# A Fourier filter and a channel MLP on one Trainium2 core: the residual operand turned by transposing DMAs instead of by TensorE and VectorE

## The chip, the cores and the metric

The kernel runs on one core of one Trainium2 chip. The metric is the device time of one execution in microseconds, and the median over runs is compared. The engines are called PE (TensorE), PEld (its weight loads), DVE (VectorE), ACT (ScalarE), POOL (GpSimd) and SP (SyncE, which here only issues DMAs).

## The reference

For each of 8 batches of 3136 positions and 256 channels:

```
X  = rfft(x, axis=1)                    # over the 3136 positions
y  = irfft(X * (filt_r + 1j*filt_i))    # one filter per frequency and channel
u  = y + ((y^T @ U) @ V)^T              # a low-rank (32) mixing over the positions
out = u + relu(u @ w_ch1) @ w_ch2       # w_ch1: 256 x 1024, w_ch2: 1024 x 256
```

Inputs and output are float32; the kernel computes in float16 with float32 sums.

## The kernel before, in words

The transform of length 3136 is split as 49 x 64 and done by matmuls. Each batch passes four stages, and then its rows pass the MLP:

- Stage 1 (`f1`, line 241; `f1_turned` for batches 0 and 1): matmuls of x with the table `ws`. ACT evicts to a tile `asb` (line 255, four buffers), and SP stores it to DRAM as `ct1` and `ct0` (lines 257 and 258).
- Stages 2 and 3 (`mid`, line 319): SP loads `ct1` and `ct0` as `a2` and `a20` (`load_a2`, lines 328 and 331), a matmul gives pz (line 384), DVE multiplies it by the filter (lines 392 to 397), a second matmul gives pe (line 345), ACT evicts it to `e3` (line 355), and SP stores it to DRAM as `ct2` (line 364, in the page as `ct<-e`).
- The rows: `load_e2` (line 412) loads `ct2` back as the 96 rows `eb`, the operand of stage 4, in three parts of two halves. `rank` (line 419) works out the low-rank term, which DVE copies into the first 32 rows of `eb` (line 438).
- Stage 4 (`s4`, line 445): matmuls of `eb` with `sv` (line 456) give u with channels on the partitions, `ut` (128 x 2 x 3136, two buffers); DVE and ACT evict it (lines 463 and 461).
- The MLP goes over the 25,088 rows of all batches in 49 groups of 512. `mm1` (line 484) gives eight blocks of the hidden layer, which ACT evicts with the relu (line 491). `mm2` (line 538) sums them over the hidden layer into a bank `pc` with rows on the partitions (line 544).

All but batch 0's stages is dealt over the MLP's steps. A step is one `mm1` block of group n and one half of an `mm2` block of group n-1; there are eight steps a group. The list `plan` names, for each step, the generators that are advanced by one piece behind it. Each engine takes its instructions in this order, and so does SP with its DMAs: one that waits holds all behind it.

```
for n, gr in enumerate(groups):
    for t in range(8):
        mm1(gr, t)
        if n:
            mm2(groups[n - 1], t)
        for gen in plan[8 * n + t]:
            next(gen, None)
```

S[b] is the first step of the group in which batch b begins: 0, 48, 96, 144, 192, 240, 288, 336, with 392 as the end. For batch b, z = S[b], and e = z - 17, z - 20 or z - 22 (b = 1, 2 to 5, 6 and 7) is where stage 3 ends. The row loads are at e - 5, e - 4 and e + 1, `rank` goes from e to e + 6, and stage 4 from e + 8 to z - 2.

The MLP's residual needs u with rows on the partitions, and `ut` has channels there. There are two ways in the kernel, chosen by `turned`:

- Groups 0 to 37: TensorE adds it, by eight matmuls of a block of `ut` with the identity into the same bank (`residual`, line 536), two more where two batches meet inside a block. DVE then copies the bank to `och` (line 561).
- Groups 38 to 48 (`FIRST_TURNED = 38`): `turn_u` transposes `ut` on DVE in blocks of 32 x 32 (line 515), SP stores the result to DRAM in four DMAs (line 520) and loads it as `tur` (line 524, in a buffer of the x tiles). DVE then adds it while it evicts the bank (line 557).

POOL's queue stores `och` to the output, and loads x for a later batch.

Of the kernel before, what the change touches and what calls it, by code (L numbers as in the profile page):

```python
# [10 lines left out]
F16 = mybir.dt.float16  # L11
# [3 lines left out]
NB = 8  # L15
# [3 lines left out]
DM = 256  # L19
# [1 line left out]
NH = 1024  # L21
GT = 512
NG = NB * SEQ // GT
FIRST_TURNED = 38

# [53 lines left out]
def kernel(  # L81
# [11 lines left out]
    nc = tc.nc  # L93
# [15 lines left out]
    sb = ctx.enter_context(tc.tile_pool(name="sb", bufs=1))  # L109
    ps = ctx.enter_context(tc.tile_pool(name="ps", bufs=2, space=bass.MemoryType.PSUM))  # L110

    def bank(tag, name, dtype=F32):

        return ps.tile([128, 512 if dtype == F32 else 1024], dtype, tag=tag, bufs=4 if tag == "z" else 2, name=name)

    def dram(t, off, dims):
        return bass.AP(tensor=t, offset=off, ap=[list(d) for d in dims])
# [88 lines left out]
    tu = eb[0:RANK, 0:12, :].rearrange("p r d -> p (r d)")  # L206
# [34 lines left out]
    def f1(b):  # L241
        for c in range(4):
            t = xt[b, c].rearrange("p (j d) -> p j d", d=DM)
            asb = sb.tile([98, 8, DM], F16, tag="asb", bufs=4, name="asb")
            for half in range(2):
                for i in range(2):
                    pf = bank("z", "pf")
                    for s in range(2):
                        j = 4 * half + 2 * i + s
                        nc.tensor.matmul(pf[0:98, 256 * s:256 * s + 256],  # L250
                                         ws[:, (8 * c + j) * 98:(8 * c + j + 1) * 98], t[:, j, :],
                                         start=(s == 0), stop=True, skip_group_check=True)
                    dst = asb[:, 4 * half + 2 * i:4 * half + 2 * i + 2, :]
                    src = pf[0:98].rearrange("p (j d) -> p j d", d=DM)
                    nc.scalar.copy(dst, src)  # L255
                    if half and i:
                        nc.sync.dma_start(dram(ct1[b], 8 * c * 96 * DM, [[DM, 96], [96 * DM, 8], [1, DM]]), asb[0:96])
                        nc.sync.dma_start(dram(ct0[b], 8 * c * DM, [[32 * DM, 2], [1, 8 * DM]]),
                                          asb[96:98].rearrange("p j d -> p (j d)"))
                    yield  # L260
# [58 lines left out]
    def mid(b, tag="z"):  # L319
        a2 = {}  # L320

        def load_a2(g):
            if b < 2:
                a2[g] = turn(b, g)
                return
            if g == 3:
                t = a20[b % 2]
                nc.sync.dma_start(t[0:64], ct0[b].ap())
            else:
                t = sb.tile([128, 8, DM], F16, tag="a2", bufs=3, name="a2")  # L330
                nc.sync.dma_start(t, dram(ct1[b], 8 * g * DM, [[24 * DM, 128], [1, 8 * DM]]))
            a2[g] = t
# [34 lines left out]
            spread_filters(0)  # L367
        for g in (0, 3, 1, 2) if b > 1 else (0, 3):
            load_a2(g)
        todo = []  # L370
        first_at = 2 if b < 2 else 6
        for i, ks in enumerate(PAIRS[:first_at] + [(0,)] + PAIRS[first_at:]):
            n = len(ks) * DM
# [7 lines left out]
            if ks[0]:  # L381
                src = a2[(ks[0] - 1) // 8]
                k = (ks[0] - 1) % 8
# [3 lines left out]
            o = 512 if ks[0] % 4 == 3 else 0  # L387
# [93 lines left out]
    def utv(b):  # L481
        return ut[b].rearrange("p h q r -> p h (q r)")
# [9 lines left out]
        gr.h.append(h)  # L492

    def turned(gr):
        return gr.n >= FIRST_TURNED

    def turn_u(gr):

        t = sb.tile([128, 4, 4, 2, 32], F16, tag="asb", bufs=4, name="tu")
        for dh in range(2):
            for b, t0, o, n in gr.seg:
                j, z = o // 32, (o + n) // 32
                while j < z:

                    k = min(z, j + 4 - j % 4) if j % 4 or z - j < 4 else z - z % 4
                    src = utv(b)[:, dh, t0 + 32 * j - o:t0 + 32 * k - o]
                    if k - j < 4:
                        dst = t[:, j % 4:j % 4 + k - j, j // 4, dh, :]  # L510
                        src = src.rearrange("p (c e) -> p c e", e=32)
                    else:
                        dst = t[:, :, j // 4:k // 4, dh, :].rearrange("p c g e -> p g c e")
                        src = src.rearrange("p (g c e) -> p g c e", c=4, e=32)
                    nc.vector.transpose(dst, src)
                    j = k
            yield
        td = nc.dram_tensor(f"tu_{gr.n}", (128, 4 * DM), F16, kind="Internal")
        for a in range(4):
            nc.sync.dma_start(dram(td, DM * a, [[4 * DM, 32], [128 * DM, 4], [1, DM]]),  # L520
                              t[32 * a:32 * a + 32].rearrange("i c g h e -> i c (g h e)"))
        yield
        gr.tu = sb.tile([128, 4, 4, 2, 32], F16, tag="x", bufs=4, name="tur")
        nc.sync.dma_start(gr.tu.rearrange("p a g h e -> p (a g h e)"), td.ap())
        yield

    def residual(gr, o, i):
        last = []
        for b, t0, so, n in gr.seg:
            a, z = max(so, 128 * i), min(so + n, 128 * i + 128)  # L530
            for dh in range(2):
                if a < z:
                    p = a - 128 * i
                    last.append((o[p:p + z - a, 128 * dh:128 * dh + 128], utv(b)[:, dh, t0 + a - so:t0 + z - so], dh))
        for d, w, dh in last:
            nc.tensor.matmul(d, w, idn, start=False, stop=(dh == 1), skip_group_check=True)  # L536

    def mm2(gr, t):
        i, half = t // 2, t % 2
        if t % 4 == 0:  # L540
            gr.pc = bank("o", "pc")
        o = gr.pc[:, 256 * (i % 2):256 * (i % 2) + 256]
        for tt in range(4 * half, 4 * half + 4):
            nc.tensor.matmul(o, gr.h[tt][:, 128 * i:128 * i + 128], w2sb[:, tt, :],  # L544
                             start=(tt == 0), stop=(tt == 7 and turned(gr)), skip_group_check=True)
        if half and not turned(gr):
            residual(gr, o, i)

        parts = {3: (0, 1), 5: (2,), 7: (3,)} if gr.n == NG - 1 else {3: (0, 1), 7: (2, 3)}
        if t not in parts:  # L550
            return
        if t == 3:
            gr.och = sb.tile([128, 4, DM], F32, tag="och", bufs=2, name="och")
        a, n = parts[t][0], len(parts[t])
        dst, src = gr.och[:, a:a + n, :], gr.pc[:, 256 * (a % 2):256 * (a % 2 + n)]
        if turned(gr):
            nc.vector.tensor_add(dst.rearrange("p g (h a e) -> p (g h) a e", h=2, a=4),  # L557
                                 src.rearrange("p (f a e) -> p f a e", a=4, e=32),
                                 gr.tu[:, :, a:a + n].rearrange("p a g h e -> p (g h) a e"))
        else:  # L560
            nc.vector.tensor_copy(dst, src.rearrange("p (j d) -> p j d", d=DM))  # L561
        if gr.n == NG - 1:
            nc.sync.dma_start(dram(out.tensor, (gr.n * GT + 128 * a) * DM, [[DM, 128], [128 * DM, n], [1, DM]]), dst)
        elif t == 7:
            nc.gpsimd.dma_start(dram(out.tensor, gr.n * GT * DM, [[DM, 128], [128 * DM, 4], [1, DM]]), gr.och)  # L565
# [3 lines left out]
    plan = [[] for _ in range(8 * NG)]  # L569

    def deal(gen, count, a, z):
        for i in range(count):
            plan[max(0, int(a + i * (z - a) / count))].append(gen)
# [6 lines left out]
    mids = [mid(0, "o")] + [mid(b) for b in range(1, NB)]  # L580
    ranks = [rank(b) for b in range(NB)]
    s4s = [s4(b) for b in range(NB)]
    turns = [turn_u(gr) for gr in groups]
# [47 lines left out]
    def loads(b, part):  # L631
        load_e2(b, part)
        yield

    for b in range(1, NB):
        a, z = S[b - 1], S[b]
        e = z - (17 if b == 1 else 20 if b < 6 else 22)
        deal(mids[b], 13, a + {1: 8, 2: -3}.get(b, -5), e - 4)
        deal(mids[b], 4, e - 4, e)
        for p, at in enumerate((e - 5, e - 4, e + 1)):  # L640
            plan[at].append(loads(b, p))
        deal(ranks[b], 6, e, e + 6)
        deal(s4s[b], 16, e + 8, z - 2)
        if b == 1:
            deal(f1s[1], 12, 1, 8)
        if b + 1 < NB:
            for c in range(4):
                plan[a + (9 + 2 * c if b == 1 else 1 + 4 * c)].append(later_x(b + 1, c))
            deal(f1s[b + 1], 16, a + (21 if b == 1 else 10), z - (13 if b == 1 else 20))

    for gr in groups:
        if turned(gr):
            for i in range(4):
                plan[8 * gr.n + (0, 1, 2, 5)[i]].append(turns[gr.n])
    for n, gr in enumerate(groups):
        for t in range(8):
            mm1(gr, t)
# [36 lines left out]
```

## Time and profile before

| | |
|---|---|
| median of 3 runs | 514.82 us (513.02 to 515.63) |
| the profiled execution | 516.74 us |
| its span in the profile | 514.9 us |
| TensorE busy, granted clock | 490.8 us (95%), 0.997 |
| DVE, ACT, POOL busy | 365.4, 377.0, 80.6 us |
| DMA: moved, mean rate | 93.99 MB, 183 GB/s |

Busy shares are of the span. A matmul's duration is the time that it takes to pass through the array, and the next begins before it ends, so the pace of matmuls is read from their starts. A wait is put down to what came last; an engine's idle time costs something only where another waits for it. A DMA is shown as issued; it lands some microseconds later, and its packets run on 16 DMA engines that all queues share.

### The profile page before, as it was taken

The numbers are of one execution on the slowest core, as the hardware profiler recorded it, in microseconds if no ns is written. First come the engines' busy times: TensorE is split into PE (matmuls) and PEld (weight loads), VectorE is DVE, ScalarE is ACT, GpSimd is POOL, SyncE is SP. The second block draws the span as 40 slices with busy tenths as digits, with TensorE's granted clock in tenths as the row PEclk, the third lists the DMA queues.
The fourth block names the chain that finished last, engine by engine and source line by source line (L and its number), as shares of the span: only waits on it lengthen the run. The fifth ranks groups of instructions, "written<-read, shape, count | busy, mean of one in ns | idle before, by whom it ended". The sixth has DMA issues, their size and how long they took to land.

```text
span 514.9 us, 11918 instructions
## 1 busy us (share of the span) xinstructions
PE 490.8 (95%) x4762; PEld 349.8 (68%) x4762; DVE 365.4 (71%) x496; ACT 377.0 (73%) x704; POOL 80.6 (16%) x122
## 2 busy tenths in 40 slices
PE   4886899999999999999999999999999999999997
PEld 4545566776777777777767777677667766676665
DVE  5886599479847986679747986679846897863432
ACT  6874779867986689667986689667895677666663
POOL 6662010012001120002001120002001000011100
PEclk9998999999999999999999999999999999999999
DMA  8987926847777386827877386836977136654454
GB/s 192 170 210 177 174 80 178 271 168 181 215 227 249 77 188 195 293 118 187 208 226 251 75 190 203 276 129 168 224 230 239 55 103 204 206 159 145 131 163 163
DMA packets 75312, 93.99 MB, mean 183 GB/s; under 512 B 5731, under 2 KB 58403, under 8 KB 75256
## 3 DMA queue, kind: packets, MB, share of 16 engines
q1 hardware_dynamic: 60552, 51.65, 33.1%
q0 software_dynamic: 14704, 41.58, 31.5%
q8 instruction: 37, 0.61, 0.5%
q14 instruction: 19, 0.16, 0.1%
HBM read 58.09 MB, written 50.66 MB: 211 GB/s over the span
## 4 chain that ended last, share of the span: by engine, by line
PE 80%; DMA 10%; DVE 4%; ACT 2%; POOL 1%; issue 1%; SPq 1%; POOLq 0%; DVEq 0%; ACTq 0%
PE pc L544 30%; PE phh L488 29%; PE pu L456 5%; PE pf L250 4%; PE pe L345 4%; PE pz L384 3%; DMA ct<-e 3%; PE pc L536 3%; DVE uv L392 2%; DMA eb<-ct 2%; DMA w2sb<-in_moe_w_ch_dram 2%; DMA x<-in_x_dram 2%; DMA fab<-in_filt_i_dram 1%; PE ph L423 1%; POOL x L128 1%
## 5 line engine op out<-in xcount | busy, mean ns | idle before, releaser
L491 ACT ACTIVATE h<-phh 128x512 f16<-128x512 f32 x392 | 235.9, 603 | 85.3 <-PE phh L488 83.8
L544 PE MATMUL pc<-w2sb,h 128*128 128x256 f16 x1568 | 233.8, 272 | 1.4 <-DMA w2sb<-in_moe_w_ch_dram 0.9
L488 PE MATMUL phh<-ut,w1sb 128*128 128x512 f16 (+7 forms) x896 | 233.3, 352 | 0.4 <-DVE ut L463 0.4
L544 PEld LDWEIGHTS <-h 128*128 128x128 f16 x1568 | 151.6, 97 | 92.2 <-issue 1.8
L392 DVE TENSOR_TENSOR uv<-pz,fab 128x1024 f16<-128x1024 f32 (+1 forms) x104 | 120.7, 1178 | 12.6 <-PE pz L384 10.5
L565 POOL DMA_DIRECT2D out_dram<-och x48 | 39.0, 813 | 402.7 <-DVE och L561 327.1
L488 PEld LDWEIGHTS <-w1sb 128*128 128x128 f16 x896 | 78.9, 97 | 19.8 <-issue 1.5
L561 DVE COPY och<-pc 128x512 f32<-128x512 f32 x76 | 52.3, 689 | 44.7 <-PE pc L536 43.5
L355 ACT CAST e<-pe 128x512 f16<-128x512 f32 x96 | 56.5, 591 | 19.4 <-PE pe L345 18.5
L463 DVE CAST ut<-pu 128x392 f16<-128x392 f32 x92 | 48.5, 558 | 19.6 <-PE pu L456 17.3
L255 ACT CAST asb<-pf 98x512 f16<-98x512 f32 x96 | 57.2, 598 | 0.2
L438 DVE COPY eb<-h 32x4096 f16<-32x4096 f16 x32 | 38.2, 1232 | 14.2 <-ACT h L435 14.1
L456 PE MATMUL pu<-sv,eb 97*128 97x49 f16 x1024 | 40.5, 187 | 5.4 <-DMA eb<-ct 5.4
L557 DVE TENSOR_TENSOR och<-pc,tur 128x512 f32<-128x512 f32 (+1 forms) x23 | 15.3, 667 | 40.4 <-PE pc L544 38.7
L345 PE MATMUL pe<-uv,m 128*128 128x512 f16 (+1 forms) x117 | 41.3, 371 | 2.4 <-DVE uv L392 1.3
L456 PEld LDWEIGHTS <-eb 97*128 97x128 f16 x1024 | 37.6, 98 | 7.2 <-issue 4.7
L536 PE MATMUL pc<-idn,ut 128*128 128x128 f16 (+1 forms) x310 | 41.9, 219 | 0.0
L384 PE MATMUL pz<-a,m 128*128 128x512 f16 x96 | 36.2, 379 | 1.3 <-DVE a L311 1.0
L250 PE MATMUL pf<-x,ws 98*98 98x256 f16 x192 | 36.6, 273 | 0.0
L536 PEld LDWEIGHTS <-ut 128*128 128x128 f16 (+1 forms) x310 | 29.6, 98 | 4.0 <-issue 0.6
L396 DVE TENSOR_TENSOR uv<-uv 64x1024 f16<-64x1024 f16 (+1 forms) x49 | 30.9, 630 | 1.7
L397 DVE TENSOR_TENSOR uv<-uv 64x1024 f16<-64x1024 f16 (+1 forms) x49 | 30.7, 627 | 0.7
(80 smaller groups left out, 262.7 us busy)
## 6 DMA issues: line engine op xcount, KB each, us to landing
out_dram<-och POOLq DMA_DIRECT2D x48, 512.0 KB, 4.1
ct<-e SPq DMA_DIRECT2D x47, 256.0 KB
eb<-ct SPq DMA_DIRECT2D x46, 256.0 KB
x<-in_x_dram POOLq DMA_DIRECT2D x28, 392.0 KB, 7.9
ct<-asb SPq DMA_DIRECT2D x24, 384.0 KB
a<-ct SPq DMA_DIRECT2D x18, 512.0 KB
tu<-tu SPq DMA_DIRECT2D x44, 64.0 KB
tur<-tu SPq DMA_DIRECT2D x11, 256.0 KB
```

Source lines behind the costliest of these rows:

```text
L250: nc.tensor.matmul(pf[0:98, 256 * s:256 * s + 256], ws[:, (8 * c + j) * 98:(8 * c + j + 1) * 98], t[:, j, :], start=(s == 0), stop=True, s ...
L255: nc.scalar.copy(dst, src)
L345: nc.tensor.matmul(pe[:, 0:n], w, uv[:, f, o:o + n], start=(f == 0), stop=(b > 0 or f == 1))
L355: nc.scalar.copy(t[:, 2 * (i % 2):2 * (i % 2) + 2, :].rearrange("p k d -> p (k d)"), pe)
L384: nc.tensor.matmul(pz, a2m, src[:, k:k + 2, :].rearrange("p k d -> p (k d)"), start=True, stop=True)
L392: nc.vector.tensor_mul(uv[:, :, o:o + n], zin, fin)
L456: nc.tensor.matmul(pu[:, NQ * i:NQ * i + NQ], eb[:, 8 * n + i, d], sv[:, 8 * g + i, :], start=(i == 0), stop=True, skip_group_check=True)
L488: nc.tensor.matmul(ph[:, o:o + n], w1sb[:, dh, 128 * t:128 * t + 128], utv(b)[:, dh, t0:t0 + n], start=(dh == 0), stop=(dh == 1), skip_gro ...
L491: nc.scalar.activation(h, ph, RELU)
L536: nc.tensor.matmul(d, w, idn, start=False, stop=(dh == 1), skip_group_check=True)
L544: nc.tensor.matmul(o, gr.h[tt][:, 128 * i:128 * i + 128], w2sb[:, tt, :], start=(tt == 0), stop=(tt == 7 and turned(gr)), skip_group_check ...
L561: nc.vector.tensor_copy(dst, src.rearrange("p (j d) -> p j d", d=DM))
```

## The change

`turned` now holds for every group that lies in one batch: 42 of the 49. The groups that span two batches (6, 12, 18, 24, 30, 36 and 42) have the residual on TensorE; group 42 had been turned before. `turn_u` no longer uses DVE or DRAM: two DMAs with a transpose, issued by SP, write 128 x 512 of `ut` each into a tile `tur` of its own (two buffers, 2 KB a partition each). It is one piece, at the first step of its group (8n), except for the third group before the one in which the next batch begins: there at e - 6 (batches 1 to 5), or e + 3 (6 and 7). A buffer of `tur` is free when DVE has added the group before the last.

`mid` for b > 1 now yields once behind its loads `load_a2`. This first piece is placed at e + 2 of the batch before (z - 12 for batch 2), behind the row loads, and was at S[b-1] - 5 (S[1] - 3 for batch 2) together with the first pair. `asb` has three buffers instead of four.

```
-            asb = sb.tile([98, 8, DM], F16, tag="asb", bufs=4, name="asb")
+            asb = sb.tile([98, 8, DM], F16, tag="asb", bufs=3, name="asb")
...
         for g in (0, 3, 1, 2) if b > 1 else (0, 3):
             load_a2(g)
+        if b > 1:
+            yield
...
     def turned(gr):
-        return gr.n >= FIRST_TURNED
+        return len(gr.seg) == 1
 
     def turn_u(gr):
-
-        t = sb.tile([128, 4, 4, 2, 32], F16, tag="asb", bufs=4, name="tu")
...
-                    nc.vector.transpose(dst, src)
...
-        gr.tu = sb.tile([128, 4, 4, 2, 32], F16, tag="x", bufs=4, name="tur")
-        nc.sync.dma_start(gr.tu.rearrange("p a g h e -> p (a g h e)"), td.ap())
+        gr.tu = sb.tile([128, 2, 4, 128], F16, tag="tur", bufs=2, name="tur")
+        for b, t0, o, n in gr.seg:
+            for dh in range(2):
+                nc.sync.dma_start(gr.tu[:, dh, :, :], utv(b)[:, dh, t0:t0 + n], transpose=True)
         yield
...
         if turned(gr):
-            nc.vector.tensor_add(dst.rearrange("p g (h a e) -> p (g h) a e", h=2, a=4),
-                                 src.rearrange("p (f a e) -> p f a e", a=4, e=32),
-                                 gr.tu[:, :, a:a + n].rearrange("p a g h e -> p (g h) a e"))
+            nc.vector.tensor_add(dst.rearrange("p g (h d) -> p g h d", h=2), src.rearrange("p (g h d) -> p g h d", h=2, d=128),
+                                 gr.tu[:, :, a:a + n, :].rearrange("p h g d -> p g h d"))
...
+    turn_at = {}
+
     for b in range(1, NB):
...
+        turn_at[z // 8 - 3] = e - 6 if b < 6 else e + 3
         deal(ranks[b], 6, e, e + 6)
+        if b + 1 < NB:
+
+            plan[z - 12 if b == 1 else e + 2].append(mids[b + 1])
...
     for gr in groups:
         if turned(gr):
-            for i in range(4):
-                plan[8 * gr.n + (0, 1, 2, 5)[i]].append(turns[gr.n])
+            plan[turn_at.get(gr.n, 8 * gr.n)].append(turns[gr.n])
```

More of the change, by code (lines that the diff above doesn't have):

```diff
@@ L23 @@
 NG = NB * SEQ // GT
-FIRST_TURNED = 38
 ORDER = np.concatenate([8 * (2 * (i % 4) + i // 4) + np.arange(8) for i in range(8)])
@@ L496, in turned @@
     def turned(gr):
-        return gr.n >= FIRST_TURNED
+        return len(gr.seg) == 1
     def turn_u(gr):
-        t = sb.tile([128, 4, 4, 2, 32], F16, tag="asb", bufs=4, name="tu")
[L502 to L514, printed above, removed]
-                    nc.vector.transpose(dst, src)
[L516 to L522, printed above, removed]
-        gr.tu = sb.tile([128, 4, 4, 2, 32], F16, tag="x", bufs=4, name="tur")
-        nc.sync.dma_start(gr.tu.rearrange("p a g h e -> p (a g h e)"), td.ap())
+        gr.tu = sb.tile([128, 2, 4, 128], F16, tag="tur", bufs=2, name="tur")
+        for b, t0, o, n in gr.seg:
+            for dh in range(2):
+                nc.sync.dma_start(gr.tu[:, dh, :, :], utv(b)[:, dh, t0:t0 + n], transpose=True)
         yield
```

## The prediction

> **What bounds the kernel now.** I read the busy time first, then the costliest groups, then the timeline where a step has the operation that the change removes, then the waits and the windows of each batch.
>
> ```profile
> PE 490.8 (95%) x4762; PEld 349.8 (68%) x4762; DVE 365.4 (71%) x496; ACT 377.0 (73%) x704; POOL 80.6 (16%) x122
> ```
>
> ```profile
> PE 80%; DMA 10%; DVE 4%; ACT 2%; POOL 1%; issue 1%; SPq 1%; POOLq 0%; DVEq 0%; ACTq 0%
> ```
>
> TensorE is busy for 95% of the span and is 80% of the chain that ended last. From 60 us on it hardly stops: in the windows of three microseconds between 78 and 330 us it is at 3.00 of 3.00 throughout. Anything taken out of its queue there should come off the time, as long as the others keep up.
>
> ```profile
> L536 PE MATMUL pc<-idn,ut 128*128 128x128 f16 (+1 forms) x310 | 41.9, 219 | 0.0
> L561 DVE COPY och<-pc 128x512 f32<-128x512 f32 x76 | 52.3, 689 | 44.7 <-PE pc L536 43.5
> L557 DVE TENSOR_TENSOR och<-pc,tur 128x512 f32<-128x512 f32 (+1 forms) x23 | 15.3, 667 | 40.4 <-PE pc L544 38.7
> ```
>
> L536 is the residual: u turned and added by a matmul with the identity. Its 219 ns are length, not pace, since matmuls overlap. The pace is read from the timeline of TensorE:
>
> ```profile
> 328.61 0.60 PE L544 MATMUL pc<-w2sb,h 128*128 128x256 f16 x4
> 329.04 0.28 PE L536 MATMUL pc<-idn,ut 128*128 128x128 f16 x2
> 329.15 0.59 PE L488 MATMUL phh<-ut,w1sb 128*128 128x512 f16 x2
> 329.59 0.60 PE L544 MATMUL pc<-w2sb,h 128*128 128x256 f16 x4
> 330.02 0.59 PE L488 MATMUL phh<-ut,w1sb 128*128 128x512 f16 x2
> 330.45 0.60 PE L544 MATMUL pc<-w2sb,h 128*128 128x256 f16 x4
> ```
>
> A step with the residual takes 329.59 - 328.61 = 0.98 us, one without 330.45 - 329.59 = 0.86. The pair occupies 329.15 - 329.04 = 0.11 us: 55 ns for one matmul.
>
> **What goes: the residual.** It is done now for groups 0 to 37: 38 x 8 matmuls, and 6 more where a batch ends inside a block of 128 rows, the 310 of the row. Afterwards only the seven groups that span two batches (6, 12, 18, 24, 30, 36, 42) have it: 7 x 8 + 8 = 64. Gone are 246 x 55 ns = 13.5 us. Group 42, which DVE turns now, gets eight of the 64.
>
> **What goes: DVE's turning.** 26 transposes of some 0.67 us and 55 DMAs, all after 426 us. In 457 to 514.9 us DVE is busy for 20.6 of 57.9 us, so nothing there is on the path: 0 us. The add of 667 ns takes the place of the copy of 689 ns: 0 us too.
>
> **What comes: 84 transposing DMAs on SP**, two of 128 KB for each of 42 groups. The trace has none, so I bound the price. From below: 512-byte packets of the hardware queue took 28 ns each on average, so 256 KB on 16 engines is 512 x 28 / 16 = 0.9 us a group. From above: if every 4 bytes went as its own packet, as the smallest of the trace did at 9 ns, 65,536 x 9 / 16 = 37 us a group. I take the nearest row: a transpose into 128 partitions takes pieces of 128 elements, 256 bytes, and the trace's 256-byte packets took 27 ns: 1024 x 27 / 16 = 1.7 us a group, 73 us in all.
>
> ```profile
> q1 hardware_dynamic: 60552, 51.65, 33.1%
> q0 software_dynamic: 14704, 41.58, 31.5%
> ```
>
> ```profile
> 111.00:168.00 57.00, 57.00 (x554) 40.57 (x553) 42.23 (x55) 43.86 (x82) 7.16 (x10) 1.00 0.68 198
> ```
>
> The DMA engines are used for 65% of the span, and in the batch from 111 to 168 us for 0.68 of it (the last but one number). Six groups of 1.7 us are 10 us more in 57: 0.86. There is room on average, up to (1 - 0.652) x 514.9 / 42 = 4.3 us a group.
>
> The Trainium skill speaks here with two voices. "VectorE: DVE Perf Modes", section "The three transpose paths", gives 1309 ns for a 128x128 block on the DMA path and 390 ns on TensorE: block after block that would be 8 x 1.309 = 10.5 us a group, an estimate, against the 0.44 us that this trace shows TensorE paying. "DMA: Bandwidth & Descriptors", section "Latency and other measured facts", gives 261 GB/s for a DMA transpose, 1.0 us a group, and the sum would stay as below. No run so far shows either; the first is taken up among the rivals.
>
> **Where the engines' rings are full: the rows.** Each batch's stage 4 (L456) waits for the rows eb, which go from the last stage-3 eviction to DRAM and back.
>
> ```profile
> PE pu L456 <- DMA eb<-ct: 5.4, 3, 3.5
> ```
>
> ```profile
> 329.14 1.16 SPq L416 DMA_DIRECT2D eb<-ct  x2
> 333.28 0.59 PE L456 MATMUL pu<-sv,eb 97*128 97x49 f16 x16 [1.25 <-DMA eb<-ct]
> ```
>
> The first half of the rows landed 2.5, 1.2, 0.6 and 0.1 us before stage 4 of batches 1 to 4 began, 1.4 before that of batch 6, and too late for 5 and 7 (stalls of 1.4 and 0.9 us). That chain is DMA time and does not shrink, while the eight steps over it lose four residual pairs, 0.44 us: batches 4 and 5 stall by about 0.4 us more each, so 0.9 us goes back. The transposes of the third group before a batch's end are issued at e - 6 (e: the end of stage 3), just ahead of the first rows. For batches 2 to 5 they wait on SP for a tur buffer, freed by an add that is recorded one step later, with row loads, ct stores and an asb store behind them. The last ct store comes six steps later, so I charge only the added traffic: 0 to 1.7 us at each of batches 1 to 5, less the slack above; I take 2 us in all (0 to 5).
>
> **A transpose behind the stage-2 loads.** These 1.5 MB now stand in SP's order right behind the rows and ahead of the next transposes. In real time they hardly move: before, SP ran ahead and issued them there anyway (330.40 behind 329.14). What they do is stand before tur. Worst is batch 6: the turning of group 33 is at e + 3, behind loads that landed between 391.4 and 395.9 us, and its add is due where DVE has its copy at 391.06. DVE would wait some 6 us with the casts of ut (L463) queued behind it. TensorE has four z banks, about 3 us of stage 4, and then stands: 3 us (0 to 5). At batches 2 to 5 the same meeting is about even: 1 us in all (0 to 4). SP itself issues 12 more DMAs a batch at 0.3 to 1.6 us (its shortest and longest now), 4 to 19 us of 57: nothing.
>
> **Engines that are full beside TensorE.** Of the 304 residual matmuls in 60 to 426 us, 185 lie in windows where DVE or ACT is busy for 2.9 us or more of three, such as these:
>
> ```profile
> 147.00:150.00 3.00, 3.00 (x27) 1.99 (x28) 0.69 (x1) 3.00 (x7) 0.00 (x0) 1.00 0.97 348
> 288.00:291.00 3.00, 3.00 (x29) 2.43 (x27) 2.92 (x4) 1.80 (x4) 0.87 (x2) 1.00 0.03 5
> ```
>
> (TensorE, its weight loads, DVE, ACT, POOL in that order.) If TensorE could gain nothing in those, 185/304 of 13.5 = 8.2 us would be lost. But each stretch is 6 to 12 us long, the gain in it is half a microsecond, and four banks take up more than that; over a batch both stand at 77% or less. I take 2 us (0 to 8).
>
> **Three asb buffers.** Stage-1 stores follow each other by about 6 us (issued at 137.50, 143.70, 149.60), so a buffer comes round after 12 us or more and its store has landed: 0 us. Were a store that late, ACT's L255 would wait and hold the z banks, 1 or 2 us a batch.
>
> **Sum.** -13.5 + 0.9 + 2 + 3 + 1 + 2 = -4.6 us. The profiled execution took 516.74 us (span 514.9 and 1.8 around it), so 512.1; the three runs have their median at 514.82, 1.9 below the profiled one, so 510.2. I predict **510.0**. Less than 0.5% (2.6 us) is about what a measurement here can't tell from no change.
>
> **Rivals.** *The gain is paced away* (0.13). If DVE and ACT hold TensorE in their full windows, 8.2 instead of 2 us go back, and the time is 514.82 + 1.6 = 516.4, within the bound. For: 185 of 304. Against: in those same windows TensorE is never without work now.
>
> *The rows come late: slower* (0.18). The transposes at e - 6 hold SP for the tur buffer and sit in the rings ahead of the ct stores and rows. If that delays the rows by d at all seven boundaries, it costs 7 x d less the slack of 5.8 us above. It decides from (13.5 + 5.8) / 7 = 2.8 us, the delay that a group's transposes bring if they hold the rings for 2.8 us instead of 1.7. At 4 us: 28 - 5.8 - 13.5 = 8.7 us slower, 523.5. For: the DMA share is about 1.0 from 147 to 153 us already. Against: 141 to 144 us, where these transposes fall, has 0.09.
>
> *The rings saturate* (0.10). Above 4.3 us a group the DMA engines become the bound. At 32-byte pieces and 9 ns each a group takes 8192 x 9 / 16 = 4.6 us: 28 more in a batch with 39 of 57 used is 67, 10 us longer in each of six, so about 575. By the skill's 1309 ns a block it would be 42 x 10.5 - 179 = 262 us longer, about 777. Against: no row that moves whole 256-byte pieces is that slow.
>
> *Full gain* is inside the forecast (0.59): with nothing given back, 501.3. Its own range is 501 to 512.2.
>
> **The numbers.** 0.59 faster, 0.13 within the bound, 0.28 slower. The range runs from 501, nothing given back, to 530, which takes in the paced case and late rows with d up to 5 us (530.5); the saturated rings and little else are left out.
>
> **What would show it.** Right: 64 matmuls at the residual's line; steps of 0.87 us; DMA share near 0.8; and DVE's add at group 33 waiting for tur. The transposes' landing times decide between the cases: under 5 us for the forecast, over 10 for the last. Late rows would show as waits of L456 for eb above 15 us in total. Wrong would be a TensorE busy all the same with steps of 0.98 us: the residual was not what paced it.

## The result, and the profile after

The changed kernel takes 532.64 us (median of 4 runs, 530.84 to 535.27), the kernel before 514.58 in the same comparison: a ratio of 1.0348 (95% interval 1.0316 to 1.038). It is slower, and outside the range. Medians, differences and ratios here and below leave out runs over 1.5% above the fastest of their kernel; the extremes in brackets are of all its runs.

The profiled execution took 533.43 us with a span of 531.6. Its page, for the parts shown of before:

```profile
PE 485.8 (91%) x4516; PEld 339.3 (64%) x4516; DVE 351.0 (66%) x470; ACT 376.1 (71%) x704; POOL 81.3 (15%) x122
PE 68%; DMA 13%; DVE 7%; ACT 4%; issue 1%; SPq 1%; POOL 0%; DVEq 0%; ACTq 0%
q1 hardware_dynamic: 98328, 56.90, 46.1%
q0 software_dynamic: 14704, 41.58, 33.3%
L536 DVE TENSOR_TENSOR och<-pc,tur 128x512 f32<-128x512 f32 (+1 forms) x85 | 58.1, 683 | 93.7 <-PE pc L523 78.2
```

246 matmuls are gone (4762 to 4516), and yet TensorE's share fell from 95 to 91%: it waits more. Of the twelve points that it lost in the chain, DMA, DVE and ACT have eight. The hardware queue moves 5 MB more in 38,000 more packets, and its share went from 33.1 to 46.1%.

The residual is now at L515 (64 matmuls), `mm1` at L489, `mm2` at L523, the add at L536, stage 4 at L457, the rows at L417, the ct stores at L363, the transposes at L503. What TensorE waits for, from the waits:

```profile
DVE och L536 <- DMA tur<-ut: 14.2, 3, 8.3
PE pu L457 <- DMA eb<-ct: 8.9, 5, 2.7
PE pu L457 <- DVE ut L464: 7.2, 2, 5.0
PE pc L523 <- DMA w2sb<-in_moe_w_ch_dram: 5.5, 1, 5.5
```

Each row is: who waited for what, us in all, times, longest. The trace gives an account of the whole difference if the gap from one matmul's start to the next is set against its columns at 2.4 a nanosecond, which is the pace of the prediction's step without the residual (2048 columns in 0.86 us). The columns' own time fell from 478.9 to 465.8 us, and the rest rose from 25.3 to 55.0: -13.1 + 29.7 = +16.6, against 16.7 of span. The 29.7 us are: stalls ahead of stage 4 of batches 1 to 7, 10.3 now and 2.3 before, +8.0; two stalls inside stage 4 where DVE waited for tur, at 404 and 463 us, +7.5; the wait for w2sb, 5.65 and 1.03, +4.6; matmuls at half clock, +3.8; four stalls of 0.74 us between stage 4 and the next stage 2, +3.0; and 2.8 in smaller gaps, most in the first 60 us.

**The rows.** The last stage-3 eviction of batch 2 and its store, from the timeline before:

```profile
148.10 0.63 ACT L355 CAST e<-pe 128x512 f16<-128x512 f32 x1
148.77 0.74 SPq L364 DMA_DIRECT2D ct<-e  x1
```

The same eviction after, among what SP does ahead of stage 4 of that batch:

```profile
150.67 3.04 SPq L503 DMA_TRANSPOSE tur<-ut  x2
153.77 1.22 SPq L417 DMA_DIRECT2D eb<-ct  x2
153.87 0.63 ACT L354 CAST e<-pe 128x512 f16<-128x512 f32 x1
155.09 0.53 SPq L363 DMA_DIRECT2D ct<-e  x1
155.66 1.17 SPq L417 DMA_DIRECT2D eb<-ct  x2
156.92 0.54 SPq L363 DMA_DIRECT2D ct<-e  x1
```

ACT had ended the last eviction at 153.87 + 0.63 = 154.50 us, and its store is issued at 156.92, 2.4 us later; before, the same store followed its eviction by 0.04 us. At batches 2 to 5 it is 2.3 to 2.5 us, at 6 and 7, where the transposes come later, 0.03. The pair holds SP for 3 us just by being issued. All transposes, from the view of the tile tur (least, median and longest ns):

```profile
L503 SPq DMA_TRANSPOSE tur<-ut x84: 1189/1489/6937, 50.5 to 519.2; - x84
```

Before, DMAs took SP 0.3 to 1.7 us.

**Group 33 and the clock.** Windows of the profile (TensorE, its weight loads, DVE, ACT and POOL busy; granted clock; DMA share, GB/s):

```profile
402.00:405.00 3.00, 2.65 (x39) 1.89 (x38) 0.00 (x0) 1.74 (x3) 0.00 (x0) 1.00 1.10 393
405.00:408.00 3.00, 0.00 (x0) 0.00 (x0) 0.00 (x0) 0.00 (x0) 0.00 (x0) 0.79 1.41 140
408.00:411.00 3.00, 1.34 (x11) 0.73 (x11) 2.56 (x6) 0.49 (x1) 0.00 (x0) 0.50 0.29 57
```

And from the timeline, what DVE and TensorE had waited for when they came back:

```profile
408.44 0.69 DVE L536 TENSOR_TENSOR och<-pc,tur 128x512 f32<-128x512 f32 x1 [8.31 <-DMA tur<-ut]
409.66 0.49 PE L457 MATMUL pu<-sv,eb 97*128 97x49 f16 x8 [5.01 <-DVE ut L464]
```

DVE stood 8.3 us for the transposes of group 33, which had gone into the rings behind 1.5 MB of stage-2 loads; with DVE stood the casts of ut, then the z banks, then TensorE for 5.2 us. When it came back it had half its clock.

**The start.** The four transposes of groups 0 and 1 run beside the load of w2sb, which lands 15.5 us after its issue instead of 10.5. The windows, with the same columns:

```profile
60.00:63.00 3.00, 0.00 (x0) 0.00 (x0) 0.00 (x0) 0.37 (x1) 0.00 (x0) 0.83 1.68 101
66.00:69.00 3.00, 3.00 (x22) 2.19 (x21) 0.85 (x2) 1.00 (x2) 0.00 (x0) 0.53 1.17 157
```

A share above 1 says that the times of packets overlap on the DMA engines, so an engine counts more than one packet at once. From 54 to 72 us the share is 1.29 on average at 134 GB/s.

### The profile page after: what moved, and what is told of

Its sections match the earlier page's. It is cut to its first block, busy times and chain, and to the rows that moved or that the text cites. A ratio compares the mean times of both kernels' runs of the same rounds, so it can differ in the third digit from the quotient of the medians.

```text
span 531.6 us, 11431 instructions
## 1 busy us (share of the span) xinstructions
PE 485.8 (91%) x4516; PEld 339.3 (64%) x4516; DVE 351.0 (66%) x470; ACT 376.1 (71%) x704; POOL 81.3 (15%) x122
## 3 DMA queue, kind: packets, MB, share of 16 engines
q1 hardware_dynamic: 98328, 56.90, 46.1%
## 4 chain that ended last, share of the span: by engine, by line
PE 68%; DMA 13%; DVE 7%; ACT 4%; issue 1%; SPq 1%; POOL 0%; DVEq 0%; ACTq 0%
PE pc L523 26%; PE phh L489 25%; PE pu L457 5%; DMA ct<-e 4%; DMA eb<-ct 4%; PE pe L344 3%; PE pz L385 3%; PE pf L249 3%; DVE uv L393 3%; DMA tur<-ut 3%; DMA w2sb<-in_moe_w_ch_dram 3%; ACT h L492 1%; ACT e L354 1%; DVE och L536 1%; ACT asb L254 1%
## 5 line engine op out<-in xcount | busy, mean ns | idle before, releaser
L523 PE MATMUL pc<-w2sb,h 128*128 128x256 f16 x1568 | 235.5, 274 | 6.0 <-DMA w2sb<-in_moe_w_ch_dram 5.5
L489 PE MATMUL phh<-ut,w1sb 128*128 128x512 f16 (+7 forms) x896 | 235.1, 354 | 0.4 <-DVE ut L464 0.4
L523 PEld LDWEIGHTS <-h 128*128 128x128 f16 x1568 | 152.5, 98 | 98.5 <-issue 8.9
L536 DVE TENSOR_TENSOR och<-pc,tur 128x512 f32<-128x512 f32 (+1 forms) x85 | 58.1, 683 | 93.7 <-PE pc L523 78.2
L489 PEld LDWEIGHTS <-w1sb 128*128 128x128 f16 x896 | 80.2, 98 | 23.7 <-issue 5.0
L457 PE MATMUL pu<-sv,eb 97*128 97x49 f16 x1024 | 40.1, 186 | 18.0 <-DMA eb<-ct 8.9
L457 PEld LDWEIGHTS <-eb 97*128 97x128 f16 x1024 | 38.1, 97 | 22.1 <-issue 14.2
L249 PEld LDWEIGHTS <-ws 98*98 98x98 f16 x192 | 22.8, 125 | 10.4 <-issue 1.7
L462 ACT CAST ut<-pu 128x392 f16<-128x392 f32 x36 | 17.5, 486 | 13.2 <-PE pu L457 10.0
L127 POOL DMA_DIRECT2D x<-in_x_dram x36 | 19.5, 546 | 6.1 <-PE pf L282 4.6
```

The costliest lines, as they stand in the source:

```text
L249: nc.tensor.matmul(pf[0:98, 256 * s:256 * s + 256], ws[:, (8 * c + j) * 98:(8 * c + j + 1) * 98], t[:, j, :], start=(s == 0), stop=True, s ...
L457: nc.tensor.matmul(pu[:, NQ * i:NQ * i + NQ], eb[:, 8 * n + i, d], sv[:, 8 * g + i, :], start=(i == 0), stop=True, skip_group_check=True)
L489: nc.tensor.matmul(ph[:, o:o + n], w1sb[:, dh, 128 * t:128 * t + 128], utv(b)[:, dh, t0:t0 + n], start=(dh == 0), stop=(dh == 1), skip_gro ...
L536: nc.vector.tensor_add(dst.rearrange("p g (h d) -> p g h d", h=2), src.rearrange("p (g h d) -> p g h d", h=2, d=128), gr.tu[:, :, a:a + n, ...
```

## The experiments

My theory: the TensorE work that went is a real gain of 13 us, and all of the loss comes from where the transposing DMAs stand: in SP's order ahead of the last ct store, in the rings behind the stage-2 loads, and beside w2sb. Against it: DVE and ACT pace the kernel (1); the bytes in the rings cost, wherever they stand (2); w2sb is late by itself (3).

**All 84 DMAs left out.** `none` is a constant tile of zeros.

```
-        gr.tu = sb.tile([128, 2, 4, 128], F16, tag="tur", bufs=2, name="tur")
-        for b, t0, o, n in gr.seg:
-            for dh in range(2):
-                nc.sync.dma_start(gr.tu[:, dh, :, :], utv(b)[:, dh, t0:t0 + n], transpose=True)
+        gr.tu = none
```

> The 84 transposing DMAs are left out; DVE adds a constant tile of zeros in their place (so the output lacks u in 42 groups). My theory: the 13.1 us of TensorE work that went are a real gain, and all of the loss comes from the DMAs (their traffic, their time on SP and the waits for them). Then about 13 us below the kernel before, 501 to 504, with the granted clock at 0.99 or more. Rival 1: DVE and ACT pace the kernel once TensorE has less to do; then 510 or more with no DMA at all.

Measured: 502.23 us (502.08 to 502.91) against 514.88, ratio 0.9755 (0.9709 to 0.9801). The engines, from its page:

```profile
PE 477.9 (95%) x4516; PEld 335.4 (67%) x4516; DVE 350.5 (70%) x471; ACT 375.3 (75%) x704; POOL 80.4 (16%) x122
```

TensorE is back at 95%. The gain of 12.7 us is there in full, so rival 1 falls: DVE and ACT, at 70 and 75%, take the faster pace. The stalls ahead of stage 4 are 2.2 us, as before the change. The run also has the earlier stage-2 loads and the three asb buffers, so these two parts cost nothing measurable. All 30.4 us between 502.23 and 532.64 come from the 84 DMAs and the waits for them.

**Plain DMAs in their place.**

```
-                nc.sync.dma_start(gr.tu[:, dh, :, :], utv(b)[:, dh, t0:t0 + n], transpose=True)
+                nc.sync.dma_start(gr.tu[:, dh, :, 0:128], utv(b)[:, dh, t0:t0 + n].rearrange("p (g e) -> p g e", e=128))
```

The tile is 144 columns wide here and the add reads 128 of them, so that the pieces stay 256 bytes.

> Each transposing DMA is replaced by a plain DMA of the same bytes in the same 512 pieces of 256 bytes, at the same place in SP's order, into a tile of the same use (u is not turned, so the values of 42 groups are wrong). Theory: what hurts is the transposing itself, 1.2 to 1.5 us of SP for each and packets that take longer beside others; a plain DMA takes 0.3 to 0.6 us of SP, so half or more of the loss goes: 508 to 522. Rival 2: bytes and places in the order are what costs (rings full, SP waiting for the tur buffer); then within 1% of the changed kernel, 528 to 536.

Measured: 525.02 us (522.69 to 527.84), ratio 1.0197 (1.0135 to 1.0259). The view of the tile tur:

```profile
L503 SPq DMA_DIRECT2D tur<-ut x84: 593/638/1618, 50.8 to 507.9; - x84
```

Between the two theories: transposing as such is 7.6 of the 30.4 us, and 22.8 stay with plain copies of the same bytes in the same places. A plain copy holds SP for 0.64 us instead of 1.49, and its 256-byte packets took 18.7 ns each instead of 29.1 on average. The median packet took 18 ns in both: of the change's packets 1.7% took over 100 ns, up to 5.1 us, and these make the higher mean. The last ct store is then 1.2 to 1.4 us late instead of 2.3 to 2.5, but the row loads land 4.4 us after their issue instead of 3.8 (means of batches 2 to 5), and the stalls ahead of stage 4 are 9.6 us in all, hardly less than 10.3. So bytes in the rings delay the rows too, as rival 2 has it. What falls is the wait for w2sb, 2.1 instead of 5.65 us, the stall at 463, and with them time at half clock.

**Three tur buffers.** A copy of the change with `bufs=3` for tur; three small tiles give up a buffer or share one to make the room.

> Three tur buffers instead of two (three small tiles share buffers to make the room; the order on all engines is the same). Theory on the rows: at e - 6 SP stands still for a tur buffer and the last ct store is issued 2.3 us after its eviction; with a third buffer it is issued within 0.5 us, the stalls of TensorE ahead of stage 4 at batches 2 to 5 fall from 1.5 to 2.9 us to under 1, and the time falls by 4 to 8 us, to 525 to 529. Rival 2 (the rings carry the rows late whatever SP does): stalls and time as in the changed kernel, 530 to 535.

Measured: 539.64 us (534.84 to 541.36), ratio 1.0491 (1.0431 to 1.0552): not faster but slower, so this part of my theory falls. SP ahead of batch 2's rows, from its timeline:

```profile
145.46 0.39 SPq L257 DMA_DIRECT2D ct<-asb  x1
145.94 3.54 SPq L503 DMA_TRANSPOSE tur<-ut  x2
149.54 1.22 SPq L417 DMA_DIRECT2D eb<-ct  x2
```

The transposes follow the asb store at once, no add being waited for, and the last ct store is still issued 2.5 to 3.7 us behind its eviction. It is the issuing that holds SP, not the buffer. The stalls ahead of stage 4 add up to 12.7 us; why they grew by 2.4 I can't say. Between 150 and 500 us TensorE also had half clock four times in this profile, at stalls of 3.1 to 4.7 us, and twice in the profile of the change.

**Groups 0 to 5 on TensorE.** `turned` holds for `gr.n > 5` only.

> Groups 0 to 5 have the residual on TensorE again, as before; the other 36 keep the transposing DMAs. Theory on the start: the four DMAs of groups 0 and 1 run beside the load of w2sb, which lands 5 us later, TensorE stands for 5.6 us and then gets half its clock for 6.8 us instead of 3.4. Without them w2sb lands within 11 us, the stall is under 1.5 us, and 48 matmuls of 55 ns come back (2.6 us): 523 to 528 us. Rival 3: the load of w2sb varies by itself, or other DMAs take the place; then 531 to 536.

Measured: 530.72 us (525.58 to 533.16), ratio 1.0293 (1.0218 to 1.0367). In the profile the wait for w2sb is 0.99 us, as the theory has it, but the time fell by 1.9 us only, with 2.6 us of matmuls put back. Stalls of the later batches, 1.8 us at batch 6's rows among them, took up the rest, and runs of the same kernel now differ by 7 us. Its time decides nothing, between 523 to 528 and 531 to 536.

**The third groups' transposes at step e.**

```
-        turn_at[z // 8 - 3] = e - 6 if b < 6 else e + 3
+        turn_at[z // 8 - 3] = e
```

> The third groups' transposing DMAs are issued at step e for all batches, six steps later than in the changed kernel for batches 1 to 5 and three earlier for 6 and 7: behind the last ct store and ahead of the last rows and the stage-2 loads, where SP only waits for that store to land. Number and bytes of the DMAs stay. Theory (SP's own time: 3.0 to 3.5 us for a group's pair, ahead of the last ct store): that store is issued within 0.8 us of its eviction instead of 2.3, the stalls ahead of stage 4 at batches 2 to 5 fall from 9.3 us in all to under 4, and the stall of 5.2 us at group 33 goes, as no stage-2 load is ahead of it: 518 to 526 us. Rival 2 (the rings): the stores and rows land that much later instead, the stalls stay, 529 to 535.

Measured: 523.20 us (521.41 to 525.69), ratio 1.018 (1.0137 to 1.0224). The same 84 DMAs, 9.4 us less. SP ahead of batch 2's rows, from its timeline:

```profile
159.07 0.59 SPq L363 DMA_DIRECT2D ct<-e  x1
159.76 0.50 SPq L256 DMA_DIRECT2D ct<-asb  x1
160.30 1.00 SPq L257 DMA_DIRECT2D ct<-asb  x1
161.40 3.37 SPq L503 DMA_TRANSPOSE tur<-ut  x2
164.87 1.17 SPq L417 DMA_DIRECT2D eb<-ct  x2
```

The last ct store is out 0.03 to 0.33 us behind its eviction, and the transposes take SP where it waited for that store anyway. The stalls ahead of stage 4 fall to 4.7 us, and those of groups 33 and 39 are gone. The gain in these stalls lies on SP: from the last eviction to the issue of the last rows it takes 5.9 us instead of 7.3 (means of batches 2 to 5), from there to stage 4 it takes 3.9 in both. Rival 2 said that place doesn't matter; it does.

**No transposes at the third groups; nor at groups 0 and 1; nor at the second groups.** Each run takes one set more out of the transposes and gives it back to TensorE:

```
-        return len(gr.seg) == 1
+        return len(gr.seg) == 1 and gr.n not in [z // 8 - 3 for z in S[1:NB]]
```

```
+        return len(gr.seg) == 1 and gr.n not in [z // 8 - 3 for z in S[1:NB]] and gr.n > 1
```

```
+        return len(gr.seg) == 1 and gr.n > 1 and gr.n not in [z // 8 - k for z in S[1:NB] for k in (2, 3)]
```

> The third group before the end of each batch (3, 9, 15, 21, 27, 33, 39) has its residual on TensorE; the other 35 keep the transposing DMAs. 56 matmuls come back, 3.1 us. Theory: rows on time as before (some 7 us less of stall), no wait for tur at groups 33 and 39 (7.5 us less) and less time at half clock (3 to 5 us): 513 to 520 us. Rival 2 (bytes in the rings): one seventh of the DMAs goes and one seventh of the loss, 2 us, against 3.1 that come back: 530 to 535.

> As the run without the third groups, and groups 0 and 1 have their residual on TensorE too, so that no transposing DMA runs beside the load of w2sb; 33 groups are turned by DMA. Theory: the stall of 5.6 us at the start and some 3 us at half clock go, 0.9 us comes back: 5 to 8 us below the run without the third groups, 507 to 513, at or below the kernel before. Rival 3 (the load of w2sb is late by itself): no more than 2 us below it.

> As the run before, and the second groups before the end of each batch (4, 10, 16, 22, 28, 34, 40), whose transposes stand behind the stage-2 loads, have their residual on TensorE too; 26 groups are turned by DMA. It puts back 3.1 us. If the meeting with the stage-2 loads still costs (waits of DVE for tur, z banks held), it is at or below the run before; if it costs nothing, it is 3 us above it.

Measured, in this order: 519.09 us (517.79 to 526.74), ratio 1.0091 (1.005 to 1.0133); 517.52 (511.5 to 528.36), 1.003 (0.9995 to 1.0064); 511.74 (508.68 to 519.84), 0.9941 (0.9909 to 0.9972). The first is in its range (just above it by the median of all runs, 520.15), and the third has its direction. The second missed: 1.6 us below the first instead of 5 to 8, which is what rival 3 gave. Its trace speaks against rival 3 all the same: w2sb landed after 11.4 us there and after 17.4 in the run before it. In the four profiles with the transposing DMAs of groups 0 and 1 it landed after 13.1 to 18.7 us, in the six without after 9.2 to 11.7. So the late landing comes from these DMAs; why the time did not follow is not shown.

From run to run the medians give the price of each set, in this order of taking them out, with its matmuls at 55 ns put back:

| groups | DMAs | fall in time, us | matmuls back, us | price of the DMAs, us |
|---|---|---|---|---|
| third before a batch's end (7) | 14 | 13.6 | 3.1 | 16.6 |
| 0 and 1 | 4 | 1.6 | 0.9 | 2.5 |
| second before a batch's end (7) | 14 | 5.8 | 3.1 | 8.9 |
| the other 26 | 52 | | | 2.5 (511.74 - 502.23 - 7.0) |

The column adds up to the 30.4 us by its making, but for rounding. What it tells is the spread: 2.4 and 1.3 us for a group at the two bad places, 0.1 for a group elsewhere, where TensorE's 0.44 us are worth saving. The table is as good as its medians, whose runs lie several us apart; the row of groups 0 and 1 is the weakest. In the profile without the second groups the four stalls of 0.74 us, 3.0 us in all, are gone too. Not every long issue is at a bad place: in the run just before it, the pair of group 20, one of the other 26, held SP for 9.08 us from 248.31 us on, and DVE waited 2.31 us for tur behind it. What stretches an issue to 7 us is open.

**Groups 0 and 1 out, the third groups at e; and then the second groups out as well.**

> The run with the third groups' transposes at step e, and groups 0 and 1 with their residual on TensorE (40 groups turned by DMA). In that run TensorE stood 8.2 us for w2sb and had half its clock for 6.8 us soon after. Theory on the start: both go, 0.9 us of matmuls come back, and the time falls by 8 to 11 us to 512 to 515; what is left above the run without any DMA is the second groups behind the stage-2 loads and the rows' share of the rings. Rival 3 (w2sb is late by itself): 520 to 524.

> As the run before it, with the second groups before each batch's end (4, 10, ..., 40) on TensorE: 33 groups turned by DMA, none of them at a place where SP, the stage-2 loads or w2sb are in the way. Against the kernel with both the second and the third groups on TensorE (26 turned, 512.0 us) it has 56 matmuls less, 3.1 us. If step e is a free place, 508 to 510; if the transposes beside the last ct store still delay the rows, 511 to 514.

> The kernel with 26 groups turned by DMA (not 0, 1, nor the second and third before each batch's end), measured again beside these two and the kernel before: 510 to 513, 0.4 to 0.8% faster than the kernel before, if the first measurement of 0.9941 (0.9909 to 0.9972) holds.

Measured: 513.75 us (507.82 to 526.67), ratio 0.9947 (0.9911 to 0.9984); 518.14 (512.54 to 529.27), 1.0042 (1.0003 to 1.0081); and again the one with 26 groups, 511.57 (508.56 to 514.72), 0.9921 (0.9895 to 0.9947). The first is in its range, 9.5 us below the run at step e with groups 0 and 1 turned, whose waits have this row:

```profile
PE pc L523 <- DMA w2sb<-in_moe_w_ch_dram: 8.0, 1, 8.0
```

Its 12 runs are 19 us apart, though, and the median of all twelve, 517.40, is above the range. In its profile, of an execution of 518.97 us, TensorE stood 5.0 us ahead of stage 4 of batch 6: the last ct store was 3.8 us late again. The second missed both its ranges, 508 to 510 and 511 to 514. Its only difference from the third is 7 groups turned at e, and it is 6.6 us slower: step e is a better place, not a free one. The kernel with 26 groups met its range. Measured twice, it is 0.6 and 0.8% below the kernel before, with intervals clear of 1; against the first of these three its lead is within the intervals.

## Why the prediction was wrong

- *The residual's 13.5 us*: right. The columns' time fell by 13.1 us, and without the DMAs the kernel gains 12.7.
- *The price of a transpose in the rings*: right. I took 256-byte packets and 1.7 us a group; the trace has 43,000 such packets, 29.1 ns each on average, so 1.9. "VectorE: DVE Perf Modes" of the Trainium skill, section "The three transpose paths", by whose 1309 ns a block it would have been 10.5 us, is not borne out for several blocks in one DMA. The 261 GB/s of "DMA: Bandwidth & Descriptors" of the Trainium skill, section "Latency and other measured facts", is not reached here: 512 packets at the mean of 29.1 ns on 16 engines make 141 GB/s, at the median of 18 ns 228, both estimates.
- *"SP itself issues 12 more DMAs a batch at 0.3 to 1.6 us ...: nothing"*: this step failed. A transpose takes SP 1.2 to 2.2 us, at times 6.9 (the longest issue before was 1.7, not 1.6), and I summed this over a batch, where there is room, instead of laying it against the one store that had none. The term for the rows, 2 us (0 to 5), was set on "the last ct store comes six steps later, so I charge only the added traffic". The stalls there grew by 8.0 us, against 2.9 with the 0.9 for shorter steps: at each of batches 2 to 5 the store left SP 2.3 to 2.5 us late, which took the slack first and stood as a stall for the rest. The 0.9 us by themselves were not seen: without the DMAs the stalls are as before. Added traffic has a part as well, by the run with plain DMAs; how much of the 8.0 us is not separated.
- *Group 33*: the mechanism is as written, wait, casts, banks; 3 us were 5.2 in its stall, 2.4 more at group 39, and half clock behind the first of them.
- *"At batches 2 to 5 the same meeting is about even: 1 us in all"*: mis-sized. Four stalls of 0.74 us stand there, 3.0 us, and the second groups' DMAs cost 8.9 us in all, by the table.
- *The start*: not in the prediction. I priced the DMAs against the mean share, 0.65; the load of w2sb ran where the share was 1.06 already (48.5 to 59 us of the profile before), and TensorE has nothing else to do.
- *The clock*: not in the prediction; 3.8 us.
- *Engines that are full beside TensorE*, 2 us, and the rival of the paced gain: wrong. With no DMAs there is no such loss to be seen.
- *Three asb buffers, the earlier loads, DVE's transposes, the adds*: nothing, as forecast.
- The rival *the rows come late* named the place, SP and the rings at e - 6, the way and the sign; it gave 523.5 at 4 us. Its delay was 2.3 to 2.5 us at batches 2 to 5, under the 2.8 from which it would have decided alone, and its sign, waits for eb above 15 us, did not come (8.9). The sum of it with the two other places decided. I had let them stand as small terms of one forecast, or left them out, though all three hang on the same thing: a DMA that is issued where its queue has no slack.

## What to carry to other kernels

Price a DMA at the place in the order where it is issued: its time on the issuing queue against the next thing on that queue that has no slack, and its landing against what stands in the rings ahead. The mean share of the DMA engines tells neither. Work taken off a saturated engine is worth its full time only if what replaces it finds such places; here 26 of the 42 groups had one, and turning only those was 0.6 and 0.8% faster than the kernel before, in two measurements.

## What the runs showed of the hardware that I had not expected

- A transposing DMA of 128 x 512 f16 takes SP 1.49 us to issue (median), a plain one in as many pieces 0.64. The landing is known for 10 of the 84: after 5.6 us (median; 2.7 to 18.4), for 10 of the plain ones after 4.0.
- The median 256-byte packet takes 18 ns in both. With transposes 734 of 43,136 packets took over 100 ns, and they have 439 of the 1,255 us that all these packets took; with plain DMAs 3 did.
- After a stall the granted clock is at half for 3.41 or 6.83 us, some of it in the stall itself. In the kernels run here, past 46 us, 14 of 15 stalls over 3.0 us were followed by it, stalls of 2.0 to 3.0 us only sometimes, shorter ones never. "TensorE: Matmul & The Clock Gate" of the Trainium skill, section "What's actually happening", has the clock halved after an idle window of about 3.4 us that runs free. The lengths agree, and a free window would explain the stall that escaped; the shorter stalls that did not escape, down to 2.0 us, don't fit a whole idle window, and no run shows why.
- While transposes ran beside the loads at the start, the DMA share went to 1.68 and the rate fell to 101 GB/s. Without any of these DMAs the highest share there was 1.22, at 164 GB/s (54 to 57 us). In the batches at full work it was 205 to 233 GB/s at 0.87 to 0.97.
